# Attention, top-1 experts and a swish layer on one core: transposes of q and k by 64x64 products, norm rounds moved to GpSimd, longer pauses in the gate's queue

## The chip, the cores and the metric

The kernel runs on one core of a Trainium2 chip. The metric is the time of one execution on the device, in microseconds. Before the change the median of three runs is 1353.53 us (1352.38 to 1356.58).

## The reference, cut to what matters

```
x = chunk_attention(q, k, v)          # 8 batches, 8 heads, 576 rows, head size 64; softmax in chunks of 64 rows
x = x.transpose(0, 2, 1, 3).reshape(4608, 512)
xn, en = x / (|x| + 1e-6), emb / (|emb| + 1e-6)
logits = xn @ en.T / tau              # 8 experts
e = argmax(logits); gate_w = softmax(logits)[e]
x = gate_w * (relu(x @ w1[e]) @ w2[e])   # 512 -> 1024 -> 512, one expert for each token
h = x @ w_in;  g = h * sigmoid(1.702 h)  # 512 -> 2048
out = g @ w_out                          # 2048 -> 512
```

All inputs and the output are float32.

## The kernel before, in words

The program has three stages. The attention stage, up to about 264 us of the profile, goes through 36 tiles of 128 token rows in a software pipeline (the loop over `n`, LATE and the dictionaries `front` and `back` set its skew). In step n it transposes k or q of the next 256-row unit on TensorE (`emit_T`, L344, k in even steps, q in odd ones) and copies the result out of the accumulation bank on ScalarE (L349), multiplies q and k of tile n (`emit_S`, L371), subtracts the row maximum on VectorE (L378, L381), takes the exponential on ScalarE (L388), transposes the probabilities of tile n-1 (L394, L401), multiplies by v for tile n-2 (L416) and divides (L424 to L428); for tile n-3 it takes the sum of squares on ScalarE (L436) and splits the row into a high and a low half (`emit_X`: L442 to L452 on VectorE, L454 and L455 on GpSimd), which SyncE stores to a scratch tensor `xs` (L461). Rows are transposed again (L468, L474, L476) and multiplied with the expert embeddings (L491). SyncE also issues the loads of q, k and v, in the program's order, between the stores.

Work on the router is cut into five batches of tiles (8, 8, 8, 6, 6). For each there are two generators in the queue `todo`: `norm` (inverse norms, by three Newton rounds in `rsqrt`, L217 to L230) and `gate` (L560 to L658: logits, maximum, one-hot rows `oh`, their running count by products with a triangle and with ones, L596 to L599, each token's place, and the softmax weight as three small integers). `drip(n)` takes n of their operations (2n in steps 29 to 32, `rate`) and is called ten times a step between the attention's operations on VectorE. After the third batch `order` finds the busiest expert and, by 24 products with one-hot rows (`lookup`, L538), the tokens of its first three tiles; with that known, SyncE loads that expert's weights and VectorE splits them (`first_split`) while the last attention tiles run. A generator that yields "pe" is about to issue a product whose operands were issued on VectorE just before; in the old `drip` the queue then passes over one call at most.

The second stage, to 671 us, runs 39 tiles of 128 gathered tokens through two products in half-precision parts; `mm2_evac` scales a tile's result and packs it, with the token's index and scale in a tail of four 32-bit words, into a row of `ys`. VectorE and ScalarE split the next expert's weights under a branch (`swap`, L962). The third stage, to the end, is the swish layer by seven-product blocks. Both are bound by TensorE.

Of the kernel before, what the change touches and what calls it, by code (L numbers as in the profile page):

```python
# [22 lines left out]
W_EXP = 7  # L23
# [11 lines left out]
def kernel(  # L35
# [173 lines left out]
    sc_i = const.tile([128, MAXT], I32, name="sc_i")  # L209

# [85 lines left out]
    def drip(n):  # L296

        n *= rate[0]
        while n > 0 and todo:
            g = todo[0]  # L300
            if g in paused:
                n -= paused.pop(g)
                continue
            try:
                if next(g) == "pe":
                    paused[g] = 8
                n -= 1
            except StopIteration:
                todo.popleft()
# [195 lines left out]
    def norm(bi):  # L505
        t0, n = batches[bi]
        ssc, y = ss_all[:, t0:t0 + n], rn_all[:, t0:t0 + n]
        yield from rsqrt(y, small("t", n, I32), small("a", n), ssc)
        nc.vector.tensor_tensor(out=y, in0=y, in1=ssc, op=ALU.mult)
        yield  # L510
        nc.vector.tensor_scalar(y, y, 1e-6, None, op0=ALU.add)
        yield
        nc.vector.reciprocal(out=y, in_=y)
        yield
# [3 lines left out]
        )  # L518
        yield
# [25 lines left out]
    def scale_of(cols, got, parts_i):  # L545
# [7 lines left out]
        )  # L553

    def gate(bi):
# [19 lines left out]
        yield  # L575
        w = small("w", n, w=NE)
# [13 lines left out]
        ex = small("ex", n, w=NE)  # L590
        nc.scalar.activation(out=ex, in_=l, func=AF.Exp)
# [42 lines left out]
        if t0 + n == NTILE:  # L634
            yield from flags()
        se = small("se", n)
        nc.vector.tensor_reduce(out=se.unsqueeze(2), in_=ex, axis=AX.X, op=ALU.add)
        yield
        nc.vector.tensor_scalar(se, se, 1e-9, None, op0=ALU.add)
        yield  # L640
        nc.vector.reciprocal(out=se, in_=se)
        yield
        nc.vector.scalar_tensor_tensor(
            out=tok_s[:, T], in0=se, scalar=2.0 ** (-2 * W_EXP), in1=is_all[:, T],
            op0=ALU.mult, op1=ALU.mult,
        )
        yield
        cb = att.tile([128, 3, 8], I32, tag="g_cb", name="g_cb")[:, :, 0:n]
        ci = tok_s[:, T].bitcast(I32)
        nc.vector.tensor_scalar(cb[:, 0], ci, 21, None, op0=ALU.logical_shift_right)  # L650
        yield
        nc.vector.tensor_scalar(
            cb[:, 1], ci, 10, 2047, op0=ALU.logical_shift_right, op1=ALU.bitwise_and
        )
        yield
        nc.vector.tensor_scalar(cb[:, 2], ci, 1023, None, op0=ALU.bitwise_and)
        yield
        nc.vector.tensor_copy(vals[:, 2:5, T], cb)  # L658
        yield
# [41 lines left out]
    def order(c):  # L701
# [42 lines left out]
        yield "pe"  # L744
# [321 lines left out]
    def mm2_evac(i):  # L1066
# [6 lines left out]
        c_i = sc_i[:, i:i + 1]  # L1073
        tail = y[:, 2 * DM:YP].bitcast(I32).rearrange("p (a two) -> p a two", two=2)
        n = (YP - 2 * DM) // 4
# [765 lines left out]
```

## Time and profile before

| | |
|---|---|
| median of 3 runs | 1353.53 us |
| profiled execution | 1351.38 us |
| its span, first to last instruction | 1349.4 us |
| TensorE busy in the span | 1246.7 us (92%) |
| VectorE | 1048.0 us (78%) |
| ScalarE | 732.8 us (54%) |
| GpSimd | 718.4 us (53%) |
| mean granted TensorE clock | 0.976 of full speed |

In the rows, PE is TensorE, PEld its weight loads, DVE VectorE, ACT ScalarE, POOL GpSimd, SP SyncE. A row of a timeline has the start in the span, the length, engine, line, operation, output and inputs; in square brackets stands how long the engine was idle before it and what ended that. Such times are taken by the hardware profiler in one execution.

### The profile page before, as it was taken

The page shows a single profiled execution, that of the slowest core. Times are in us where ns is not written, and L with a number is a line of the kernel's source. Part 1 is how long each engine was busy: PE and PEld are TensorE (multiplying, and loading weights), DVE is VectorE, ACT ScalarE, POOL GpSimd, SP SyncE. Part 2 cuts the span into 40 slices and gives each one's busy share as a digit, 9 for nine tenths or more (in the row PEclk, how much of TensorE's full clock was granted, in tenths as well). Part 3 has the DMA queues.
Part 4 walks back from the last instruction along what each step waited for, and adds up shares of the span by engine and source line. Part 5 has one row for each costly group of instructions (what it writes and reads, how often), then busy time and mean ns, then how long its engine had stood idle before and what let it go on. Part 6 is the DMA issues. An engine that isn't in the chain of part 4 may idle for free. (4 is left out here: it accounts for less than half of the span.)

```text
span 1349.4 us, 35343 instructions
## 1 busy us (share of the span) xinstructions
PE 1246.7 (92%) x14192; PEld 1027.2 (76%) x14192; DVE 1048.0 (78%) x1872; ACT 732.8 (54%) x1301; POOL 718.4 (53%) x652
## 2 busy tenths in 40 slices
PE   6777767899999999999899999999999999999997
PEld 4666656677676666667588888888888888888886
DVE  4688888878988778886678696968687896968681
ACT  7899855235544545554463645545454645455452
POOL 1455543142444254543167575757667675757664
PEclk9999877999999999999999999999999999999999
DMA  9999635668665759885507162544526062534413
GB/s 197 233 242 230 160 129 131 181 181 229 191 182 174 212 161 274 266 253 133 151 15 212 58 183 99 129 154 94 188 39 226 19 205 77 157 125 125 157 42 116
DMA packets 218454, 213.62 MB, mean 158 GB/s; under 512 B 127320, under 2 KB 171352, under 8 KB 218272
## 3 DMA queue, kind: packets, MB, share of 16 engines
q1 hardware_dynamic: 204880, 184.17, 51.0%
q0 software_dynamic: 6000, 19.67, 4.3%
q10 hardware_dynamic: 7392, 7.36, 1.6%
q8 instruction: 114, 1.87, 0.6%
q14 instruction: 68, 0.56, 0.2%
HBM read 154.98 MB, written 36.52 MB: 142 GB/s over the span
## 5 line engine op out<-in xcount | busy, mean ns | idle before, releaser
L1536 PEld LDWEIGHTS <-wS 128*128 128x128 f16 x3024 | 296.2, 98 | 48.9 <-issue 9.7
L1029 PEld LDWEIGHTS <-w1HL 128*128 128x128 f16 x3744 | 216.9, 99 | 24.1 <-DVEq L962 6.7
L1029 PE MATMUL ph<-xTm,w1HL 128*128 128x128 f16 x3744 | 223.0, 222 | 12.2 <-DVEq L962 5.5
L1064 PE MATMUL py<-w2HL,hT 128*128 128x512 f16 x912 | 203.9, 379 | 6.0 <-DVEq L962 3.4
L1064 PEld LDWEIGHTS <-hT 128*128 128x128 f16 x936 | 89.9, 98 | 109.1 <-issue 8.0
L1089 ACT ACTIVATE y<-py,ysc 128x512 f16<-128x512 f32 x38 | 26.1, 687 | 142.8 <-DVE ysc L1086 142.8
L1004 POOL DMA_INDIRECT xg<-xs,id_i x39 | 44.3, 1135 | 107.6 <-DMA xTm<-xg 70.0
L1536 PEld LDWEIGHTS <-w2HL 128*128 128x128 f16 x864 | 84.6, 98 | 10.6
L1536 PEld LDWEIGHTS <-w1HL 128*128 128x128 f16 x864 | 84.5, 98 | 9.8
L454 POOL TENSOR_TENSOR x<-x,sx_all 128x512 f32<-128x512 f32 x33 | 34.3, 1039 | 107.3 <-DVE rd L424 41.9
L1256 POOL TENSOR_TENSOR wS<-d_f,wS 128x512 f16<-128x512 f32 x28 | 37.0, 1339 | 73.4 <-ACT wS L1255 44.5
L1562 ACT ACTIVATE zA<-zA 128x512 f32<-128x512 f32 x72 | 45.3, 628 | 53.2 <-DVE zA L1559 26.9
L1403 POOL TENSOR_TENSOR w1HL<-zA,w1HL 128x512 f16<-128x512 f32 x36 | 48.5, 1346 | 43.6 <-ACT w1HL L1399 39.7
L1396 DVE TENSOR_TENSOR zA<-zA 128x512 f32<-128x512 f32 x72 | 65.6, 910 | 1.2
L1037 DVE SCALAR_TENSOR_TENSOR hT<-ph,hT 128x512 f16<-128x512 f32 x78 | 51.4, 684 | 14.8 <-ACT hT L1036 14.7
L1036 ACT ACTIVATE hT<-ph 128x512 f16<-128x512 f32 x78 | 44.2, 594 | 30.0 <-PE ph L1029 30.0
L1536 PE MATMUL pd<-stg,wS 128*128 128x256 f16 x456 | 54.5, 272 | 2.2 <-ACT stgB L1399 2.2
L1697 POOL DMA_INDIRECT out_dram<-hT,idc x36 | 35.4, 983 | 35.7 <-ACT hT L1692 32.6
L1536 PE MATMUL pa<-stg,wS 128*128 128x256 f16 x432 | 51.7, 273 | 1.5 <-ACT stgB L1399 1.5
L1090 DVE SCALAR_TENSOR_TENSOR y<-py,ysc,y 128x512 f16<-128x512 f32 x38 | 28.5, 751 | 28.8 <-ACT y L1089 28.8
L1536 PE MATMUL pb<-stg,wS 128*128 128x256 f16 x408 | 48.9, 272 | 1.5 <-ACT stgB L1399 1.5
L349 ACT ACTIVATE kuT<-tp 64x512 f32<-64x512 f32 x72 | 45.2, 628 | 8.8 <-PE tp L344 7.9
(408 smaller groups left out, 3134.4 us busy)
## 6 DMA issues: line engine op xcount, KB each, us to landing
ring<-wod SPq DMA_DIRECT2D x63, 1024.0 KB, 5.1
stg<-in_moe_w_dram SPq DMA_DIRECT2D x14, 1024.0 KB, 6.9
stgB<-in_moe_w_dram SPq DMA_DIRECT2D x14, 1024.0 KB, 6.8
ys<-y SPq DMA_DIRECT2D x39, 258.0 KB, 3.2
vt<-in_v_dram SPq DMA_DIRECT2D x64, 144.0 KB, 5.7
xs<-xr SPq DMA_DIRECT2D x36, 256.0 KB, 5.6
raw_o<-in_moe_w_in_dram SPq DMA_DIRECT2D x16, 512.0 KB, 4.3
raw_o<-in_moe_w_out_dram SPq DMA_DIRECT2D x16, 512.0 KB, 3.8
```

The lines of the kernel that those rows point to most:

```text
L349: lambda r=r, p=p, dst=dst: nc.scalar.activation(out=dst[:, :, r], in_=p[r * 64:(r + 1) * 64], func=AF.Copy)
L1004: nc.gpsimd.indirect_dma_start(out=xg[:, :], out_offset=None, in_=src, in_offset=bass.IndirectOffsetOnAxis(ap=id_i[:, i:i + 1], axis=0),)
L1029: nc.tensor.matmul(p[:, f % 4], wt[:, c, fs], xT[:, a, :], start=(c == 0 and a == 0 and wt is w1H), stop=(c == KD - 1 and wt is w1L),)
L1036: nc.scalar.activation(out=hi, in_=p, func=AF.Relu)
L1037: nc.vector.scalar_tensor_tensor(out=lo, in0=p, scalar=0.0, in1=hi, op0=ALU.max, op1=ALU.subtract)
L1064: nc.tensor.matmul(p, hT[:, a, :], wt[:, c, :], start=st, stop=sp)
L1256: nc.gpsimd.tensor_tensor(out=L_, in0=f, in1=H_, op=ALU.subtract)
L1396: nc.vector.tensor_tensor(out=o, in0=x, in1=p, op=op)
L1403: eng.tensor_tensor(out=lo, in0=x, in1=hi, op=ALU.subtract)
L1536: nc.tensor.matmul(dst, lhs(a, k, ab), rhs(b, k), start=first and ab == abs_[0] and k == 0 and m == 0, stop=(k == n - 1 and m == 2), skip_ ...
L1562: nc.scalar.activation(out=z, in_=z, func=AF.Sigmoid, scale=1.702 * 2.0 ** -G_EXP)
L1697: disjoint("out", nc.gpsimd.indirect_dma_start(out=out[:, :], out_offset=bass.IndirectOffsetOnAxis(ap=id_t[j][0][:, 2 * h + t, 0:1], axis= ...
```

## The change

Four parts. The transposes of k and q are now products with a quarter of the identity, 64 rows by 64 columns, ordered so that all of a row half's results lie in one bank; two ScalarE copies of 128 partitions take the place of four of 64. The first four batches' Newton rounds, with the two operations after them, run on GpSimd, and the queue then pauses for eight calls of `drip` (`"far"`); `"pe"` pauses for three. The weight operations of a gate, for all batches but the last, stand right behind the one-hot rows, ahead of the product (`weights`). In `mm2_evac` the tail is written by single-column operations, and the two halves of the token's scale are split once (`sc_m`, `sc_e`) when the scale is found.

```
         n *= rate[0]
         while n > 0 and todo:
             g = todo[0]
-            if g in paused:
-                n -= paused.pop(g)
+            n -= 1
+            if paused.get(g, 0) > 0:
+                paused[g] -= 1
                 continue
             try:
-                if next(g) == "pe":
-                    paused[g] = 8
-                n -= 1
+                r = next(g)
+                if r in ("pe", "far"):
+                    paused[g] = (3 if r == "pe" else 8) * rate[0]
             except StopIteration:
+                n += 1
                 todo.popleft()
...
-        for h2 in range(2):
-            p = ps.tile([128, HP, 128], F32, tag="A", name="tp", bufs=2)
-            for hp in range(HP):
-                nc.tensor.transpose(
-                    p[:, hp, :], src[:, 2 * hp + h2].rearrange("p r d -> p (r d)"), identF
+        p = [ps.tile([128, QR, HP, 64], F32, tag="A", name="tp", bufs=2) for _ in range(2)]
+        for hp in range(HP):
+            for r in range(QR):
+                for a in range(2):
+                    rows = slice(a * 64, (a + 1) * 64)
+                    for h2 in range(2):
+                        nc.tensor.matmul(
+                            p[a][h2 * 64:(h2 + 1) * 64, r, hp, :], src[rows, 2 * hp + h2, r, :],
+                            identF[rows, rows], start=True, stop=True,
+                        )
+        for a in range(2):
+            dst = qkT[u, nm][:, :, a * 128:(a + 1) * 128].rearrange("p hp (i r) -> p hp i r", r=QR)
+            evacs.append([
+                lambda a=a, dst=dst: nc.scalar.activation(
+                    out=dst, in_=p[a].rearrange("p r hp i -> p hp i r"), func=AF.Copy
                 )
-            dst = qkT[u, nm][h2 * 64:(h2 + 1) * 64].rearrange("p hp (c r) -> p hp r c", r=QR)
-            evacs.append([
-                lambda r=r, p=p, dst=dst: nc.scalar.activation(
-                    out=dst[:, :, r], in_=p[r * 64:(r + 1) * 64], func=AF.Copy
-                )
-                for r in range(2)
             ])
...
+        if bi + 1 < len(batches):
+            gp = nc.gpsimd
+            t, a, h = small("t", n, I32), small("a", n), small("h", n)
+            nc.vector.tensor_scalar(t, ssc.bitcast(I32), 1, None, op0=ALU.logical_shift_right)
+            yield
+            nc.vector.tensor_scalar(y.bitcast(I32), t, -1.0, 1597463007.0, op0=ALU.mult, op1=ALU.add)
+            gp.tensor_scalar(h, ssc, -0.5, None, op0=ALU.mult)
+            for _ in range(3):
+                gp.tensor_tensor(out=a, in0=h, in1=y, op=ALU.mult)
+                gp.tensor_tensor(out=a, in0=a, in1=y, op=ALU.mult)
+                gp.tensor_scalar(a, a, 1.5, None, op0=ALU.add)
+                gp.tensor_tensor(out=y, in0=y, in1=a, op=ALU.mult)
+            gp.tensor_tensor(out=y, in0=y, in1=ssc, op=ALU.mult)
+            gp.tensor_scalar(y, y, 1e-6, None, op0=ALU.add)
+            yield "far"
+        else:
+            yield from rsqrt(y, small("t", n, I32), small("a", n), ssc)
...
+        nc.vector.tensor_scalar(
+            sc_m[:, cols], sc_i[:, cols], MAN_BITS, BIAS << 23, op0=ALU.bitwise_and, op1=ALU.bitwise_or
+        )
+        nc.vector.tensor_scalar(sc_e[:, cols].bitcast(I32), sc_i[:, cols], EXP_BITS, None, op0=ALU.bitwise_and)
+        nc.vector.tensor_scalar(
+            sc_e[:, cols], sc_e[:, cols].bitcast(I32), float(BIAS << 23), None, op0=ALU.add
+        )
...
+        if t0 + n < NTILE:
+            yield from weights(T, n, ex)
         yield "pe"
...
-        yield "pe"
+        yield "far"
         p0 = gb[:, 304:304 + 5 * NSURE].rearrange("p (a i) -> p a i", a=5)
         lookup(p0, lambda t: v0[:, :, t], NPART)
...
-        nc.vector.tensor_scalar(si[:, 3:4], c_i, EXP_BITS, None, op0=ALU.bitwise_and)
-        nc.vector.tensor_copy(tail[:, :, 0], id_i[:, i:i + 1].to_broadcast([128, n]))
+        for a in range(0, tail.shape[1], 2):
+            nc.vector.tensor_scalar(tail[:, a:a + 1], id_i[:, i:i + 1], 0, None, op0=ALU.bitwise_or)
...
-        nc.vector.scalar_tensor_tensor(
-            out=si[:, 2:3], in0=c_i, scalar=MAN_BITS, in1=si[:, 1:2], op0=ALU.bitwise_and, op1=ALU.bitwise_or
-        )
+        nc.vector.tensor_scalar(s[:, 2:3], s[:, 1:2], sc_m[:, i:i + 1].bitcast(F32), None, op0=ALU.mult)
...
-        nc.vector.scalar_tensor_tensor(
-            out=tail[:, :, 1], in0=si[:, 3:4].to_broadcast([128, n]), scalar=float(BIAS << 23),
-            in1=si[:, 1:2].to_broadcast([128, n]), op0=ALU.add, op1=ALU.subtract,
-        )
+        for a in range(1, tail.shape[1], 2):
+            nc.vector.tensor_scalar(
+                tail[:, a:a + 1], si[:, 1:2], -1.0, sc_e[:, i:i + 1], op0=ALU.mult, op1=ALU.add
+            )
```

How the order on the engines changes is shown at three places. First VectorE at the third batch's gate, in steps 29 of both programs, from the one-hot rows on (`g_oh`; `g_sm` and `cum` are their counts, `g_se`, `tok_s` and `g_cb` the weight, the rows with `sx_all`, `xr` and `rd` the attention's). Before:

```order
L586 TENSOR_TENSOR g_oh<-g_w,g_mw 128x64
L447 TENSOR_SCALAR sx_all<-si_all 128x1
L452 TENSOR_SCALAR xr<-x,sx_all 128x512
L603 TENSOR_REDUCE g_sm<-g_oh 128x8
L607 TENSOR_TENSOR cum<-cum,g_sm 128x8
L424 TENSOR_SCALAR rd<-db 128x8
L685 TENSOR_TENSOR cnt<-gb,io_eR 128x8
L613 TENSOR_TENSOR g_po<-gb,g_oh 128x64
```

After:

```order
L645 TENSOR_TENSOR g_oh<-g_w,g_mw 128x64
L455 TENSOR_SCALAR sx_all<-si_all 128x1
L588 TENSOR_REDUCE g_se<-g_ex 128x8
L590 TENSOR_SCALAR g_se<-g_se 128x8
L460 TENSOR_SCALAR xr<-x,sx_all 128x512
L592 RECIPROCAL g_se<-g_se 128x8
L594 SCALAR_TENSOR_TENSOR tok_s<-g_se,is_all 128x8
L601 TENSOR_SCALAR g_cb<-tok_s 128x8
L603 TENSOR_SCALAR g_cb<-tok_s 128x8
L432 TENSOR_SCALAR rd<-db 128x8
L607 TENSOR_SCALAR g_cb<-tok_s 128x8
L609 CAST vals<-g_cb 128x3x8
```

The weight operations fill the place behind the one-hot rows, and the counts stand in step 30, behind that step's row maximum.

Second TensorE, from that gate's last products on (`ptp` and `db` are the attention's, `tp` the transposes). Before:

```order
L394 MATMUL ptp<-identF,P 128x128 x4
L416 MATMUL db<-vt_91,PT 64x65 x16
L683 LDWEIGHTS ones_120
L683 MATMUL gb<-cum,ones_120 128x8
L344 MATMUL tp<-identF,ku 128x128 x8
```

After:

```order
L402 MATMUL ptp<-identF,P 128x128 x4
L424 MATMUL db<-vt_91,PT 64x65 x16
L720 LDWEIGHTS ones_120
L720 MATMUL gb<-cum,ones_120 128x8
L351 MATMUL tp<-identF,qu 64x64 x32
```

The gate's products are followed by a transpose of k before and of q after: they moved by one step, to step 30; and eight transposes became 32 calls.

Third GpSimd at the end of the first batch (`x` and `xr` are a tile's two large operations). Before:

```order
L454 TENSOR_TENSOR x<-x,sx_all 128x512
L455 TENSOR_TENSOR xr<-x,xr 128x512
L454 TENSOR_TENSOR x<-x,sx_all 128x512
L455 TENSOR_TENSOR xr<-x,xr 128x512
L454 TENSOR_TENSOR x<-x,sx_all 128x512
```

After:

```order
L462 TENSOR_TENSOR x<-x,sx_all 128x512
L463 TENSOR_TENSOR xr<-x,xr 128x512
L527 TENSOR_SCALAR g_h<-ss_all 128x8
L529 TENSOR_TENSOR g_a<-g_h,rn_all 128x8
L530 TENSOR_TENSOR g_a<-g_a,rn_all 128x8
L531 TENSOR_SCALAR g_a<-g_a 128x8
L532 TENSOR_TENSOR rn_all<-rn_all,g_a 128x8
```

The round L529 to L532 stands there three times, and L533 and L534 behind it, ahead of the next tile's `x`.

## Rows read from the trace of the kernel before

**Rows 1.** busy us (instructions) by stretch: PE, PEld, DVE, ACT, POOL; clock, DMA share, GB/s

```profile
67.40:107.50 40.10, 30.90 (x747) 24.72 (x747) 34.10 (x110) 37.28 (x70) 22.52 (x24) 1.00 1.10 242
107.50:146.50 39.00, 30.75 (x746) 24.65 (x745) 34.18 (x109) 37.11 (x70) 22.52 (x24) 1.00 1.15 234
152.06:188.85 36.79, 24.02 (x499) 20.27 (x494) 28.65 (x99) 23.87 (x45) 15.69 (x18) 0.77 0.17 50
188.85:200.83 11.98, 7.05 (x162) 5.65 (x152) 10.80 (x29) 8.21 (x17) 7.28 (x6) 0.65 0.75 273
264.00:671.00 407.00, 389.75 (x4305) 282.89 (x4306) 329.61 (x569) 196.61 (x337) 163.79 (x137) 0.99 0.70 204
671.00:1349.00 678.00, 658.92 (x5978) 585.00 (x5976) 513.47 (x650) 346.72 (x615) 447.62 (x384) 0.99 0.40 121
```

**Rows 2.** the same view for line L381 alone, one of it per tile

```profile
58.00:152.00 94.00, 13.11 (x19) 1.00 1.12 241
152.06:188.85 36.79, 3.44 (x5) 0.77 0.17 50
188.85:200.83 11.98, 1.38 (x2) 0.65 0.75 273
```

**Rows 3.** issues of transfers, 152 to 187 us: count, size, median us to landing

```profile
xs<-xr SPq DMA_DIRECT2D x5, 256.0 KB, 2.0
```

**Rows 4.** issues of transfers, 60 to 150 us

```profile
xs<-xr SPq DMA_DIRECT2D x19, 256.0 KB, 6.5
```

**Rows 5.** timeline of PE, 150 to 176 us, two rows

```profile
159.55 0.21 PE L596 MATMUL gb<-g_oh,tri 128*128 128x64 f16 x1 [3.37 <-DVE g_oh L586]
...
175.88 0.79 PE L538 MATMUL gb<-v,raw_o 128*128 128x15 f16 x24 [6.06 <-DVE v L740]
```

**Rows 6.** ACT groups, 107.5 to 146.5 us: count | busy us, mean ns | idle

```profile
L349 ACT ACTIVATE quT<-tp 64x512 f32<-64x512 f32 x17 | 10.7, 629 | 0.2
...
L401 ACT ACTIVATE PT<-ptp 128x512 f32<-128x512 f32 x8 | 4.8, 595 | 0.1
L474 ACT ACTIVATE xTa<-sp 128x1024 f16<-128x1024 f16 x4 | 4.1, 1024 | 0.1
```

**Rows 7.** timeline of all engines, 96 to 112 us, two rows

```profile
96.18 0.69 PE L371 MATMUL sp<-kuT,quT 64*64 64x64 f32 x32
...
99.19 0.66 PE L344 MATMUL tp<-identF,ku 128*128 128x128 f32 x4
```

**Rows 8.** DVE groups, 182.6 to 192 us (the fourth batch's norm)

```profile
L230 DVE SCALAR_TENSOR_TENSOR rn_all<-g_a,rn_all 128x6 f32<-128x6 f32 x3 | 1.4, 450 | 0.1
L224 DVE SCALAR_TENSOR_TENSOR g_a<-rn_all,ss_all 128x6 f32<-128x6 f32 x3 | 1.2, 402 | 0.1
...
L228 DVE TENSOR_TENSOR g_a<-g_a,rn_all 128x6 f32<-128x6 f32 x3 | 0.5, 166 | 0.1
...
L511 DVE TENSOR_SCALAR rn_all<-rn_all 128x6 f32<-128x6 f32 x1 | 0.2, 160 | 0.0
L509 DVE TENSOR_TENSOR rn_all<-rn_all,ss_all 128x6 f32<-128x6 f32 x1 | 0.2, 154 | 0.0
```

**Rows 9.** POOL groups over the whole span

```profile
L455 POOL TENSOR_TENSOR xr<-x,xr 128x512 f16<-128x512 f32 x33 | 38.8, 1176 | 2.6
...
L454 POOL TENSOR_TENSOR x<-x,sx_all 128x512 f32<-128x512 f32 x33 | 34.3, 1039 | 107.3 <-DVE rd L424 41.9 <-DVE xr L452 11.0 <-DVE g_t L217 9.8
...
L629 POOL TENSOR_SCALAR raw_o<-io_k,slot 128x128 f16<-128x128 f16 x32 | 20.8, 669 | 19.8 <-DVE slot L626 19.8
...
L1696 POOL MEMSET gap<- 128x1 f32 x36 | 3.8, 106 | 0.0
```

**Rows 10.** lines L1077 and L1078: shortest/median/longest ns, first to last start

```profile
L1077 DVE TENSOR_SCALAR ysc<-sc_i x39: 140/154/154, 241.9 to 661.6; 128x1 int32<-128x1 int32 x39
L1078 DVE COPY y<-id_i x39: 153/159/4056, 242.0 to 661.6; 128x2 int32<-128x2 int32 x39
```

**Rows 11.** waits, 264 to 671 us: total us, times, longest

```profile
PE ph L1029 <- DVEq L962: 5.5, 7, 1.7
```

More of the change, by code (lines that the diff above doesn't have):

```diff
@@ L209 @@
     sc_i = const.tile([128, MAXT], I32, name="sc_i")
+    sc_m = const.tile([128, MAXT], I32, name="sc_m")
+    sc_e = const.tile([128, MAXT], F32, name="sc_e")
     tau_sb = const.tile([128, 1], F32, name="tau_sb")
@@ L507, in norm @@
         ssc, y = ss_all[:, t0:t0 + n], rn_all[:, t0:t0 + n]
[L508 to L514, printed above, removed]
         isx = is_all[:, t0:t0 + n]
@@ L518, in norm @@
         )
+        yield
[3 more added lines that the diff above has]
+            nc.vector.tensor_scalar(t, ssc.bitcast(I32), 1, None, op0=ALU.logical_shift_right)
+            yield
+            nc.vector.tensor_scalar(y.bitcast(I32), t, -1.0, 1597463007.0, op0=ALU.mult, op1=ALU.add)
[10 more added lines that the diff above has]
+            yield from rsqrt(y, small("t", n, I32), small("a", n), ssc)
+            nc.vector.tensor_tensor(out=y, in0=y, in1=ssc, op=ALU.mult)
+            yield
+            nc.vector.tensor_scalar(y, y, 1e-6, None, op0=ALU.add)
+            yield
+        nc.vector.reciprocal(out=y, in_=y)
         yield
@@ L553, in scale_of, with weights @@
         )
+        nc.vector.tensor_scalar(
[5 more added lines that the diff above has]
+        )
+    def weights(T, n, ex):
+        se = small("se", n)
+        nc.vector.tensor_reduce(out=se.unsqueeze(2), in_=ex, axis=AX.X, op=ALU.add)
+        yield
+        nc.vector.tensor_scalar(se, se, 1e-9, None, op0=ALU.add)
+        yield
+        nc.vector.reciprocal(out=se, in_=se)
+        yield
+        nc.vector.scalar_tensor_tensor(
+            out=tok_s[:, T], in0=se, scalar=2.0 ** (-2 * W_EXP), in1=is_all[:, T],
+            op0=ALU.mult, op1=ALU.mult,
+        )
+        yield
+        cb = att.tile([128, 3, 8], I32, tag="g_cb", name="g_cb")[:, :, 0:n]
+        ci = tok_s[:, T].bitcast(I32)
+        nc.vector.tensor_scalar(cb[:, 0], ci, 21, None, op0=ALU.logical_shift_right)
+        yield
+        nc.vector.tensor_scalar(
+            cb[:, 1], ci, 10, 2047, op0=ALU.logical_shift_right, op1=ALU.bitwise_and
+        )
+        yield
+        nc.vector.tensor_scalar(cb[:, 2], ci, 1023, None, op0=ALU.bitwise_and)
+        yield
+        nc.vector.tensor_copy(vals[:, 2:5, T], cb)
+        yield
     def gate(bi):
@@ L575, in gate @@
         yield
+        ex = small("ex", n, w=NE)
+        nc.scalar.activation(out=ex, in_=l, func=AF.Exp)
         w = small("w", n, w=NE)
@@ L589, in gate @@
         yield
-        ex = small("ex", n, w=NE)
-        nc.scalar.activation(out=ex, in_=l, func=AF.Exp)
+        if t0 + n < NTILE:
+            yield from weights(T, n, ex)
         yield "pe"
@@ L635, in gate @@
             yield from flags()
[L636 to L642, printed above, removed]
-        nc.vector.scalar_tensor_tensor(
-            out=tok_s[:, T], in0=se, scalar=2.0 ** (-2 * W_EXP), in1=is_all[:, T],
-            op0=ALU.mult, op1=ALU.mult,
-        )
[L647 to L653, printed above, removed]
-        )
[L655 to L659, printed above, removed]
+        if t0 + n == NTILE:
+            yield from weights(T, n, ex)
         if t0 + n == NPART:
@@ L1092, in mm2_evac @@
         )
-        nc.vector.scalar_tensor_tensor(
-            out=tail[:, :, 1], in0=si[:, 3:4].to_broadcast([128, n]), scalar=float(BIAS << 23),
-            in1=si[:, 1:2].to_broadcast([128, n]), op0=ALU.add, op1=ALU.subtract,
-        )
+        for a in range(1, tail.shape[1], 2):
+            nc.vector.tensor_scalar(
+                tail[:, a:a + 1], si[:, 1:2], -1.0, sc_e[:, i:i + 1], op0=ALU.mult, op1=ALU.add
+            )
         if i < NSURE:
```

5 lines of the change are left out of this document (1 added, 4 removed).

## The prediction

> **What bounds the kernel now.** I read the busy times by stage first. From 671 us to the end TensorE is busy 658.92 of 678 us, from 264 to 671 us 389.75 of 407 [rows 1]: those two stages, 1085 of 1349.4 us, are TensorE's, and what other engines save there is worth at most the 17.25 us that TensorE idles in the first of them. Everything else in the change lies in the attention stage before 264 us. There the reader is to count tiles: the 128-row score subtraction (L381) runs once per tile, 19 times between 58 and 152 us, so a tile takes 94.0 / 19 = 4.95 us; then 5 tiles take 36.79 us (7.36 each) and 2 take 11.98 [rows 2]. These are two regimes.
>
> In the first one I take the two stretches of exactly eight tiles, 67.40 to 146.50 us, 79.1 us together. ScalarE is busy 74.4 of them (94%), VectorE 68.3 (86%), TensorE 61.65 (78%), GpSimd 45.0 [rows 1]. ScalarE sets the pace, but two others are close. The DMA column reads 1.10 and 1.15, 242 and 234 GB/s [rows 1], and a 256 KB store of the token rows, landed 2.0 us after its issue when nothing else is loaded, needs 6.5 us here [rows 3, 4]: the transfers queue behind each other all the time, so I treat some 238 GB/s as what this mix of transfers reaches.
>
> In the second regime no loads of q, k and v are left (50 GB/s) and no engine is near full: VectorE is busy 28.65 of 36.79 us, so it idles 8.1 [rows 1]. The idle time comes from the gate: TensorE, in order, stands 3.37 us before the product over the one-hot rows and 6.06 us before the 24 products that look up the first expert's tokens, each until VectorE is done with a chain that was issued only a few steps earlier [rows 5]; behind that product stand the next tiles' scores, which VectorE needs.
>
> **The change, part by part.**
>
> *q and k by 64x64 products.* Per tile (one of k or q is transposed per tile) four ScalarE copies of 64x512 at 0.629 us [rows 6] become two of 128x512. Nothing in the trace copies from such a strided bank; the nearest rows are 0.595 us for a contiguous 128x512 and 0.629 for the old copy, the far one 1.024 for 128x1024 elements [rows 6]. I take 0.65, with 0.6 and 1.02 as ends: 2.52 - 1.30 = 1.2 us of ScalarE per tile saved (0.5 to 1.3). ScalarE falls from 4.65 to about 3.45 us a tile. On TensorE eight 128x128 passes, 0.66 us per four, so 1.3 us, become 32 calls of 64x64. The score products have that shape and use the same four quarters of the array: 16 calls, shown as 32 matmuls, take 0.69 us [rows 7]. So 32 calls take 1.38: TensorE pays about 0.1 us more, 3.95 a tile. If the quarters did not run beside each other it would be worse; that is a rival below.
>
> *Newton rounds on GpSimd.* Of each of the first four batches' norms eleven VectorE operations go. In the fourth they are 1.4 + 1.2 + 0.5 + 0.2 + 0.2 = 3.5 us [rows 8], 0.44 us a tile: VectorE falls from 4.27 to 3.83. GpSimd gets 15 small operations instead. The trace has no arithmetic on 128x8 there: its memset of 128x1 takes 0.106 us, its compare over 128x128 0.669 [rows 9]. I take 0.2 us, near the small end since eight columns are near one, so 3 us per batch. They stand behind the tile's two large operations (1.04 + 1.18 us [rows 9]), of which about 1.2 us are left when the seed is written, and VectorE's reciprocal comes one tile later: 4.5 - 1.2 = 3.3 us are there for 15 operations, 0.22 each. At 0.2 VectorE waits hardly at all; I charge 0.5 us in all. At 0.669 it would stand 6.7 us in each of three batches (the fourth has two tiles between), 20 us, with the x and score work of every later tile queued behind it. The Trainium skill, page "GPSIMD Engine Reference", section "Engine selection", speaks against this move: it sends elementwise work to VectorE because GpSimd takes about twice as long for two inputs. By that rule an operation takes an estimated 0.33 us instead of VectorE's 0.166, 5 us per batch, 1.7 us of waiting in three batches, and the sum would be 5 us poorer.
>
> *Loads.* With ScalarE at 3.45, VectorE at 3.83 and TensorE at 3.95 the engines would allow about 4.1 us a tile. A tile needs three 256 KB inputs and one 256 KB store, 1.05 MB by the shapes, so at 238 GB/s the transfers need 4.41 us. I take 4.5 us a tile: 19 tiles x (4.95 - 4.5) = **8.5 us** saved. Ends: 0 if the queue of loads already holds the stage, and 19 x (4.95 - 4.1) = 16 if loads issued ahead are enough.
>
> *Real pauses and the moved weight operations.* The same VectorE operations are issued, so nothing of their busy time goes; only waits do. The one-hot product now stands one tile later, the weight operations fill the steps between, and the look-up comes a tile after its operands. What hides it: VectorE always has the attention's own work. Of the 8.1 us of VectorE idle time in the five tiles I count half, 4 us, as gone (0 to 8.1), since the order after the count product is still a chain of small operations. The fourth batch's norm (3.5 us) is also in this VectorE-bound stretch, less three new operations for the split scale, 0.45: 3 us. Together **7 us** (3 to 11). What is late next is VectorE itself: the gate's own operations stay. The last batch keeps its place behind the last row tile, so the start of the expert stage only moves forward with the rest. On SyncE the first expert's weight loads stand behind the same tile's store as before.
>
> *Expert results (mm2_evac).* Seven small operations become eight. The copy of the token index has a median of 159 ns but takes up to 4056; the tensor_scalar just before it, of the form that replaces it, never took over 154 [rows 10]. VectorE gains, TensorE only where it waits for VectorE's branch at a new expert, 5.5 us in 7 waits [rows 11]. I count **0.5 us** (0 to 4).
>
> Sum: -8.5 - 7 - 0.5 + 0.5 = -15.5 us. The profiled execution took 1351.4 us (span 1349.4), the median of the runs is 1353.5, 2.1 above. So 1335.9 for an execution like the profiled one and **1338** beside the median.
>
> **Rivals.**
> 1. *The loads hold the stage.* For: the store's landing is three times the undisturbed one through the whole stretch, and all loads of q and k stand on SyncE ahead of the 23rd tile's store. Against: between 60 and 150 us nothing on TensorE waits for a load. Then the first 150 us give 2 us instead of 8.5, and the sum is -9: 1344.5.
> 2. *Slower: GpSimd's rounds arrive late.* VectorE's reciprocal waits with all attention work behind it. At 0.669 us an operation: 20 us, -15.5 + 20: 1358. It decides from (3.3 + 5.2) / 15 = 0.57 us an operation, where three waits of 5.2 us eat the 15.5. Against: eight columns are far from 128. A kindred price: were the 64x64 calls to run one after the other, TensorE would need over 5 us a tile, and the stage would be some 10 us longer.
> 3. *Nothing is left: VectorE and GpSimd hold each other up.* VectorE's first Newton operation with two inputs takes 0.4 us in the mean against 0.166 for its like, next to running GpSimd work [rows 8]; 15 more GpSimd operations may hold VectorE's others in the same way, up to 3 us in each of four batches, 12 us: 1350. The Trainium skill, "SBUF — State Buffer", section "Who interferes with whom", has the rule: a VectorE operation with two SBUF inputs and a GpSimd one that reads SBUF exclude each other, and the later one stands for the whole of the first. By it the trace's slow first rounds are explained, and this rival's 12 us are the upper end.
> 4. *More than I count.* Loads issued ahead carry the stage at 4.2 us a tile (14 us), and VectorE's idle time in the gate goes almost wholly (10): 1329.
>
> **How the numbers follow.** Forecast 0.50, loads 0.24, slower 0.07, hold-up 0.07, more 0.12. About 0.3%, 4 us, is what a measurement of this kernel can tell from no change, so faster means under 1349.5. Forecast and rival 4 lie there wholly, rival 1 mostly (0.20): 0.82. The same gets the rest of rival 1 and most of rival 3, 0.10; slower 0.08. The range runs from rival 4 to just past rival 1 and to rival 3's 1350: 1328 to 1350; the forecast's own is 1331 to 1345.
>
> **What would show it.** After the change: ScalarE under 80% busy between the 9th and 28th tile, copies of q and k two per tile at about 0.65 us, a tile in 4.3 to 4.7 us there; the 32 calls in about 1.4 us; no TensorE wait over 1.5 us before the one-hot product and the look-up; 15 GpSimd operations of about 0.2 us, and no wait of VectorE's reciprocal on them; the two tiles that now end at 200.83 us done about 13 us earlier; the experts' stage and the last one of equal length. I am wrong if a tile still takes 4.9 us with ScalarE idle (loads), if the reciprocal waits (rival 2), or if the gain before 264 us is given back behind it.

## The result: slower by 13 us

The changed kernel takes 1368.07 us in the median of 4 runs (1365.37 to 1370.42), the kernel before, beside it, 1355.05 (1352.38 to 1357.32): a ratio of 1.0095, 95% interval 1.0075 to 1.0116. The prediction, 1338 us and faster, was wrong. The profiled execution takes 1365.37 us, its span is 1363.6, 14.2 more than before.

### The profile page after: what moved, and what is told of

Its sections match the earlier page's. It is cut to its first block, busy times and chain, and to the rows that moved or that the text cites. A ratio compares the mean times of both kernels' runs of the same rounds, so it can differ in the third digit from the quotient of the medians.

```text
span 1363.6 us, 39324 instructions
## 1 busy us (share of the span) xinstructions
PE 1252.9 (92%) x16208; PEld 1039.0 (76%) x16208; DVE 1023.2 (75%) x1873; ACT 684.9 (50%) x1229; POOL 732.2 (54%) x712
## 5 line engine op out<-in xcount | busy, mean ns | idle before, releaser
L1066 PE MATMUL ph<-xTm,w1HL 128*128 128x128 f16 x3744 | 220.2, 220 | 11.3 <-DVEq L999 7.3
L1569 PEld LDWEIGHTS <-w2HL 128*128 128x128 f16 x864 | 84.5, 98 | 10.6
L386 DVE TENSOR_REDUCE mx<-sp 128x8 f32<-128x512 f32 x36 | 24.7, 686 | 53.9 <-PE sp L379 53.9
```

The costliest lines, as they stand in the source:

```text
L1066: nc.tensor.matmul(p[:, f % 4], wt[:, c, fs], xT[:, a, :], start=(c == 0 and a == 0 and wt is w1H), stop=(c == KD - 1 and wt is w1L),)
L1569: nc.tensor.matmul(dst, lhs(a, k, ab), rhs(b, k), start=first and ab == abs_[0] and k == 0 and m == 0, stop=(k == n - 1 and m == 2), skip_ ...
```

## The profile after

The windows by tile come first, the score subtraction (now L389) alone, one per tile (window, length, busy of VectorE and count, granted clock, DMA share, GB/s). They answer to [rows 2]:

```profile
65.00:173.20 108.20, 13.12 (x19) 0.92 0.87 204
173.20:203.54 30.34, 3.43 (x5) 0.89 0.16 56
203.54:216.76 13.22, 1.38 (x2) 0.76 0.71 249
```

The same 19 tiles take 108.2 us instead of 94.0, 5.7 each; the next five take 30.3 instead of 36.8. So the second regime won 6.4 us, as it should, and the first one lost 14; 7.0 more are lost ahead of it (the window of the same tiles starts at 65.00 instead of 58.00), and the last two tiles lose 1.2. All engines, for 15 tiles of the first regime and for the two later stages (the columns of [rows 1]):

```profile
74.22:114.05 39.83, 30.77 (x1046) 25.79 (x1044) 29.04 (x86) 22.20 (x46) 22.04 (x35) 0.91 0.99 217
114.05:162.20 48.15, 35.25 (x1194) 30.35 (x1194) 32.35 (x98) 27.85 (x56) 26.51 (x41) 0.89 0.80 195
278.00:685.00 407.00, 390.48 (x4338) 283.88 (x4336) 309.70 (x615) 197.84 (x338) 164.10 (x137) 0.99 0.70 205
685.00:1363.00 678.00, 659.68 (x5983) 585.48 (x5980) 514.04 (x650) 346.56 (x615) 448.17 (x384) 0.99 0.40 121
```

The experts and the last stage are as long as before: the experts take 449 us from their first product to their last, 451 before (they begin at 211 us in the kernel before, ahead of the 264 us at which their stage was cut). In the first regime ScalarE fell from 94% busy to 56 and 58%, VectorE from 86 to 73 and 67%, and TensorE too, from 78 to 77 and 73%, with 60% more matmuls. Nothing is full, and the granted clock, 1.00 before, is 0.91 and 0.89. TensorE's busy time per tile rose from 3.85 to 4.40 us at that clock. m1_burst below has TensorE's stops of the kind shown next at a granted clock of 1.00, so a lower clock is not needed for them; what it adds here no run shows. Who waits then, 60 to 165 us (total us, times, longest):

```profile
DVE mx L386 <- PE sp L379: 25.0, 14, 3.8
...
PE tp L351 <- issue: 10.4, 9, 2.4
...
PE sp L379 <- issue: 7.1, 4, 2.5
...
DVE rn_all L542 <- POOL rn_all L534: 1.6, 1, 1.6
```

VectorE waits 25 us for scores, and TensorE stands ahead of transposes and scores with "issue" as the cause: it waits for nothing that the profile shows. One such place in the timeline of TensorE:

```profile
92.69 0.66 PE L402 MATMUL ptp<-identF,P 128*128 128x128 f32 x4
93.27 0.70 PE L424 MATMUL db<-vt,PT 64*64 64x65 f32 x32
93.79 1.05 PE L351 MATMUL tp<-identF,qu 64*64 64x64 f32 x57
97.25 0.34 PE L351 MATMUL tp<-identF,qu 64*64 64x64 f32 x7 [2.41 <-issue]
97.52 0.36 PE L499 MATMUL gb<-enT,xTa 128*128 128x16 f16 x8
```

The reader is to look at x57 and x7: the stop of 2.41 us comes after 57 of the 64 matmuls of one transpose, between two that have the same inputs and the same bank half. No load, buffer or engine can hold the 58th alone. What is left is the instruction itself. The queues of transfers show a kind for that; over 16 tiles (67.4 to 146.5 us before, 74.22 to 166.7 after; packets, MB, share), before and after:

```profile
q8 instruction: 12, 0.20, 1.2%
```

```profile
q8 instruction: 19, 0.31, 1.6%
```

A packet is 16,384 bytes. A tile has 93 matmuls and as many weight loads before, 149 and 149 after: 16 tiles are some 3,000 and 4,780 instructions, so about 250 to a packet (the burst below gives 258; 256 is taken from here on). In the trace's transfer records of the changed kernel they come one after the other, 5.0 us apart between 70 and 150 us (6.5 before). The stops hang on them: between 60 and 165 us TensorE has 19 with "issue" as the cause, 22.2 us together, and each of the 19 ends 1.2 to 1.7 us after the end of such a packet. One packet starts at 94.49 and takes 1.40 us; the stop above ends at 97.25, 1.36 us later. In the kernel before there is no such stop in these tiles.

Of the rest, ScalarE's copies of k and q (shortest/median/longest ns) and GpSimd's small operations are what was expected, 0.58 to 0.60 and 0.20 to 0.24 us:

```profile
L358 ACT ACTIVATE quT<-tp x16: 575/598/606, 74.4 to 165.7; 128x512 f32<-128x512 f32 x16
L358 ACT ACTIVATE kuT<-tp x16: 576/584/597, 77.7 to 161.9; 128x512 f32<-128x512 f32 x16
```

```profile
L531 POOL TENSOR_SCALAR g_a<-g_a 128x8 f32<-128x8 f32 x6 | 1.4, 238 | 0.5
...
L532 POOL TENSOR_TENSOR rn_all<-rn_all,g_a 128x8 f32<-128x8 f32 x6 | 1.2, 202 | 0.5
```

TensorE's waits between 155 and 220 us, to be read against [rows 5]: the two on the one-hot rows and the look-up, 3.37 and 6.06 us, are gone; the longest that are left stand before the products with v and before the logits.

```profile
PE db L424 <- DVE x L436: 7.2, 4, 3.5
PE gb L499 <- ACT xTa L482: 5.3, 1, 5.3
```

The index copy of the experts' results answers to [rows 10] and never takes over 155 ns now; TensorE's wait for VectorE's branch, to [rows 11], is no shorter (7.3 us in 6):

```profile
L1113 DVE TENSOR_SCALAR y<-id_i x78: 136/145/155, 257.9 to 676.0; 128x1 int32<-128x1 int32 x78
```

```profile
PE ph L1066 <- DVEq L999: 7.3, 6, 2.5
```

## The experiments

The leading theory, A: 128 instructions of TensorE a tile in place of 16 need more packets than arrive in time. "Tile" in the table is the distance between the row maxima of the 12th and the 28th tile divided by 16, "six" that from the 30th to the 36th; ratios are to the kernel before on the same chip; the runs are spread over several chips. A tile is read from one profiled execution, and that leaves some 0.1 us open: m1_burst is the kernel before, unchanged, up to its added products, and its tile is 5.07 us where the profile of before has 4.95.

| kernel | median us | ratio, 95% | tile us | six us |
|---|---|---|---|---|
| before | 1355.05 | | 4.95 | 44.5 |
| after | 1368.07 | 1.0095 (1.0075 to 1.0116) | 5.78 | 39.4 |
| x1_old_T | 1349.15 | 0.9966 (0.9953 to 0.9979) | 5.18 | 38.3 |
| x2_new_T | 1375.72 | 1.0154 (1.0130 to 1.0178) | 5.81 | 44.6 |
| x3_16calls | 1346.76 | 0.9954 (0.9938 to 0.9970) | 5.06 | 39.4 |
| x7_after_few_v | 1356.55 | 1.0026 (1.0005 to 1.0047) | 5.41 | 39.4 |
| x6_16calls_few_v | 1341.08 | 0.9899 (0.9874 to 0.9925) | 4.81 | 39.2 |
| x8_mix | 1344.91 | 0.9931 (0.9908 to 0.9954) | 4.95 | 39.3 |
| x9_mix_few_v | 1342.75 | 0.9927 (0.9903 to 0.9950) | 4.93 | 38.2 |
| x10_before_few_v | 1349.80 | 0.9967 (0.9954 to 0.9980) | 4.91 | 45.0 |
| p1_pauses | 1346.34 | 0.9944 (0.9922 to 0.9965) | 5.14 | 38.1 |
| p2_pauses_norms | 1352.91 | 0.9993 (0.9975 to 1.0010) | 5.27 | 39.4 |
| x11_pauses_mix | 1347.24 | 0.9950 (0.9934 to 0.9967) | 5.09 | 38.5 |
| y6_mix_XT_late | 1360.02 | 1.0033 (1.0019 to 1.0047) | 5.67 | 40.5 |
| y7_oldT_XT_late | 1367.45 | 1.0092 (1.0078 to 1.0106) | 6.10 | 40.5 |
| y9_mix_XT_late_few_v | 1357.03 | 1.0019 (1.0006 to 1.0033) | 5.80 | 40.0 |
| y4_mix_xTa_ACT | 1343.63 | 0.9921 (0.9909 to 0.9934) | 4.85 | 37.5 |
| z1_XT_late_xTa_ACT | 1344.93 | 0.9945 (0.9926 to 0.9964) | 5.11 | 37.5 |
| z2_no_gps_norms | 1338.22 | 0.9888 (0.9866 to 0.9910) | 4.93 | 36.3 |

**Without the products, and with nothing else.** x1_old_T puts the old `emit_T` back into the changed kernel, x2_new_T puts the new one alone into the kernel before.

> The changed kernel with q and k transposed as before (8 transposes of 128x128 and four copies per tile); all other parts of the change kept. Theory A (the 32 calls are 128 instructions of TensorE per tile where there were 16, and these arrive too late; TensorE stands with nothing that the profile shows): the stops without a visible cause between 60 and 165 us, some 20 us in the changed kernel, fall under 3 us, a tile takes 4.9 us again, the gate's stretch keeps its 5 us, and the time is 1346 to 1352, a ratio of 0.994 to 0.998. Theory D (GpSimd's rounds, the pauses or the moved weight operations delay the stage): the time stays 1360 to 1370, ratio over 1.004.

> The kernel before with nothing but the 64x64 products for q and k. Theory A: the same stops as in the changed kernel, a tile at 5.6 to 5.9 us instead of 4.95 between the 12th and the 28th, about 20 us lost before 160 us: 1368 to 1378, ratio 1.010 to 1.017. Theory D: no stops, ScalarE relieved: 1342 to 1352, ratio 0.991 to 0.998.

Times and stops are as theory A has them: 0.9966 and 1.0154. The tile of x1_old_T, 5.18 us, is not back at the 4.9 expected, though its stops are gone. The products alone cost 20.8 us, the other three parts together save 4.6; that makes 16.2 where the changed kernel lost 13, which the intervals allow. TensorE's waits, 60 to 150 us, in x2_new_T:

```profile
PE tp L347 <- issue: 6.3, 4, 3.3
PE db L420 <- issue: 4.3, 4, 1.8
PE sp L375 <- issue: 3.5, 2, 2.0
```

In x1_old_T, 60 to 165 us, TensorE has no wait with "issue" as the cause; it waits for ScalarE's copies, as before the change, and for VectorE:

```profile
PE tp L348 <- ACT kuT L353: 7.1, 10, 0.8
PE db L420 <- DVE x L432: 6.9, 7, 1.4
```

**Half the instructions.** x3_16calls keeps the two copies, with 64 instructions a tile:

```
-        for hp in range(HP):
-            for r in range(QR):
-                for a in range(2):
-                    rows = slice(a * 64, (a + 1) * 64)
-                    for h2 in range(2):
-                        nc.tensor.matmul(
-                            p[a][h2 * 64:(h2 + 1) * 64, r, hp, :], src[rows, 2 * hp + h2, r, :],
-                            identF[rows, rows], start=True, stop=True,
...
+        for r in range(QR):
+            p = ps.tile([128, HP, 128], F32, tag="A", name="tp", bufs=2)
+            for hp in range(HP):
+                for h2 in range(2):
+                    nc.tensor.matmul(
+                        p[h2 * 64:(h2 + 1) * 64, hp, :], src[:, 2 * hp + h2, r, :], identF,
+                        start=True, stop=True,
...
```

> The changed kernel with 16 products of 128 rows by 64 columns per tile in place of 32 of 64 by 64: 64 instructions of TensorE instead of 128 (16 before), the same two copies per tile on ScalarE. Theory A (the number of instructions counts): the stops without a visible cause fall from 20 us to under 7, a tile takes 4.6 to 5.1 us, 1345 to 1356, ratio 0.993 to 1.001. Theory B (products in quarters or halves of the array cost TensorE more time than their count says, whatever the number of instructions): a tile stays at 5.6 us or more, 1365 to 1375, ratio over 1.007.

0.9954 and 5.06 us a tile, as theory A expects; TensorE's stops without a cause fall to 2.3 us between 70 and 150 us (17.2 in the changed kernel):

```profile
PE db L419 <- issue: 1.2, 1, 1.2
PE sp L374 <- issue: 1.1, 2, 0.6
```

B falls.

**The cost by itself.** m1_burst runs the products behind the last store, 24 groups of 32 calls in the quiet (L1820), then 24 beside loads:

```
+    burst(24, dst)
...
+    for n in range(18):
+        load_w(NG, n % 7)
+    burst(24, dst)
```

> The kernel before, with the products of the 64x64 transposes measured by themselves behind its last store: 24 groups of 32 calls (128 instructions of TensorE each) with no transfer beside them, then 24 more while eighteen loads of 1 MB run. Theory A: TensorE stands between stretches of some 256 instructions, so a group takes more than the 1.4 us of its matmuls, 1.6 to 2.0 us in the quiet part and over 2.2 us beside the loads; instruction packets of 16 KB come one after the other, one per 256 instructions. Theory B: the matmuls themselves take over 2 us a group in both parts, with no stops. Neither: 1.4 us a group in both parts.

It ran once. The first 24 groups take 42.1 us, 1.75 each, the others 62.4, 2.60 each. Windows in the quiet and beside the loads (columns of [rows 1]), and TensorE's waits ahead of 1384.5 us:

```profile
1343.00:1384.50 41.50, 23.68 (x1423) 21.86 (x1414) 0.00 (x0) 0.00 (x0) 0.00 (x0) 1.00 0.06 16
1386.00:1431.00 45.00, 22.44 (x938) 21.14 (x928) 0.00 (x0) 0.00 (x0) 0.00 (x0) 0.73 1.01 403
```

```profile
PE pd L1820 <- issue: 16.6, 11, 1.9
```

In the quiet TensorE works through 2,837 instructions, 11.1 packets, in 23.68 us, 2.1 us a packet, so a group of 32 calls by itself is 1.07 us; the stops are 11, one per packet. The packets' queue shows 11 in these 41.5 us, 3.7 us apart in the records. Beside 403 GB/s of loads it is 8 in the 43 us from 1388 to 1431, 5.9 us apart in the mean, with stops up to 4.4 us:

```profile
q8 instruction: 8, 0.13, 1.2%
```

So with nothing else to wait for, the packets set the pace, and loads stretch it from 3.7 to 5.9 us. The records show which part they stretch: from TensorE's going on to the start of the next packet it is 1.1 us in the quiet, 2.4 in the changed kernel and 3.7 beside the loads (medians); the packet itself takes 1.1 to 1.2 us and the time from its end to the next instruction 1.2 to 1.7, in all three. A part of the 2.60 us goes with the clock: a group is busy 1.53 us at a granted clock of 0.73 and 1.07 at 1.00. The Trainium skill, page "Runtime: NRT & Kernel Launch", section "Instruction fetch mechanics", says that an engine's instructions are refilled in 16 KiB blocks of 256, and that crossing a block's boundary is "mostly hidden". The trace agrees with the block; on the hiding the measurement decides: 1.5 us per block are not hidden here in the quiet, and more beside loads.

**The changed kernel with a quarter less to load.** x7_after_few_v (and the other few_v kernels):

```
-            nc.sync.dma_start(out=dst, in_=src)
+            if v_n[0] < NV * H:
+                nc.sync.dma_start(out=dst, in_=src)
```

> The changed kernel itself with, of v, only the first three batch entries loaded: a quarter less to transfer per tile. Theory A (TensorE's instructions come by the transfer engines' rings, 3.55 us per packet in the quiet, 6.2 beside full loads): packets come every 4.0 to 4.5 us instead of 4.8, a tile falls from 5.8 us to 4.9 to 5.4, and the time to 1353 to 1362, ratio 0.999 to 1.006, though no engine has less to do. Theory B (the products' shape costs it): a tile stays at 5.6 to 5.8, 1364 to 1370, ratio over 1.007.

The time is as expected of A, some 9 us less than the changed kernel's (1.0026 against 1.0095) with the same work on every engine; the tile, 5.41 us, and the packets, 4.6 us apart, fall as they should and end just past the range written down. The time by itself is weak evidence, since the kernel before gains 4.5 us from the same edit (x10_before_few_v below); the tile and the packets, which came 5.78 and 5.0 us apart, are the better one.

**What the relief of ScalarE is worth, the instructions mended.** x8_mix takes the 16 products for k and the old transposes for q:

```
+    def emit_T(u, nm):
+        return (emit_Tk if nm == "ku" else emit_Tq)(u, nm)
```

> The changed kernel with k by the 16 products of 128 rows by 64 columns and q by the 8 transposes and four copies of before, so that TensorE and ScalarE share the cost. If the engines set the pace of a tile (ScalarE some 4.0 us busy, TensorE 4.3, VectorE 4.0, and at most 40 extra calls), a tile takes 4.5 to 4.75 us between the 12th and the 28th, and the time is 1338 to 1344, ratio 0.988 to 0.993. If the loads of q, k and v hold the stage (rival 1 of the prediction), a tile stays at 4.95 to 5.1 us and the time at 1345 to 1350, ratio 0.994 to 0.998.

> The kernel with 16 products of 128 rows by 64 columns and, of v, only the first three batch entries loaded (later ones compute with these): 0.79 instead of 1.05 MB per tile. If the loads hold the stage, a tile falls from 5.06 us to 4.4 to 4.7, and the time by 6 to 10 us, to 1336 to 1341, ratio 0.988 to 0.992. If the engines do (TensorE 4.6 us busy per tile), a tile stays at 4.85 to 5.1 and the time at 1343 to 1348.

> The kernel that has k by 16 products and q by 8 transposes, with only the first three batch entries of v loaded: of the 18.6 MB that it moves between 70 and 146 us about 4.5 MB go. No engine of it is over 88% busy there. If the transfers hold a tile at 4.95 us (18.6 MB at 245 GB/s are 76 us), it falls to 4.35 to 4.65 us, and the time to 1335 to 1341, ratio 0.986 to 0.990. If the chain from engine to engine holds it, the tile stays at 4.8 to 4.95 and the time at 1341 to 1346.

> The kernel before with only the first three batch entries of v loaded. If ScalarE (94% busy) sets the pace of a tile, as the prediction has it, the tile stays at 4.8 to 4.95 us and the time at 1349 to 1354, ratio 0.996 to 1.0. If the transfers do, it falls to 4.65 to 4.75, as far as ScalarE's 4.65 us allow, and the time to 1344 to 1349, ratio 0.993 to 0.996.

x8_mix has one stop without a cause between 70 and 150 us, of 0.3 us, and no engine over 88% busy, and yet the tile is 4.95, the upper of the two outcomes written down, where loads were held to be the cause; its time lies between the two. The loads are not it: x9_mix_few_v moves 172 instead of 245 GB/s, and its tile is 4.93. The same window, 70 to 146 us, of x8_mix and x9_mix_few_v:

```profile
70.00:146.00 76.00, 66.57 (x1616) 53.55 (x1614) 64.70 (x191) 62.22 (x119) 49.18 (x69) 1.00 1.12 245
```

```profile
70.00:146.00 76.00, 65.98 (x1618) 53.59 (x1620) 65.63 (x192) 62.72 (x120) 49.43 (x71) 1.00 0.62 172
```

x10_before_few_v says the same of the kernel before: 4.91, as with ScalarE as its bound; that its time falls by 4.5 us all the same is not explained, and its profiled execution, the slowest of its ten, shows no stage shorter. Of the two kernels with fewer instructions than the change, x6_16calls_few_v alone gains from fewer loads (0.9899 against 0.9954, and 4.81 against 5.06 us a tile), but its instructions, 0.9 packets a tile, can arrive sooner too, so it does not tell the two apart.

That 4.95 us is also the tile of the kernel before does not mean that the relief is worth nothing, since x8_mix holds the other parts of the change as well. The kernel that differs from it in the transposes alone is x1_old_T: 5.18 us a tile and 0.9966 against 0.9931, some 5 us, with intervals that just overlap. The same edit between p1_pauses and x11_pauses_mix, below, takes 0.05 us off the tile and nothing off the time. So the relief won 0.05 to 0.23 us a tile where 0.45 were counted.

**The parts of the router.** p1_pauses has the real pauses and moved weight operations alone; p2_pauses_norms adds the rounds on GpSimd (`norm` of the change); x11_pauses_mix adds the shared transposes to p1_pauses.

> The kernel before with the real pauses and the moved weight operations alone: no GpSimd rounds, no 64x64 products, results of the experts as before. By the prediction's terms: 4 us from the waits of the gate's stretch, the fourth norm's 3 us not: 1348 to 1351, ratio 0.996 to 0.998, the stretch of six tiles from 44.5 to 40 to 42 us. If the gain of 4.6 us that the changed kernel without the products shows is the norms' instead, this one stays within 0.2% of before.

> The real pauses and moved weight operations with the Newton rounds of the norms on GpSimd. By the prediction's terms (the fourth norm's 3 us off VectorE, 0.5 us of waiting in all) 2 to 3 us better than the pauses alone, 0.992 to 0.993. If GpSimd's rounds hold VectorE's reciprocal up by 1.6 us per batch, as the traces show in places, no better or up to 3 us poorer: 0.994 to 0.997.

> The real pauses and moved weight operations with k by 16 products and q by 8 transposes; the norms and the experts' results as before. If the gains of the two parts add (pauses alone 0.9944, transposes shared between the engines some 4 us on top), 1339 to 1344, ratio 0.989 to 0.993. If the transfers hold the stage whatever the engines do, no better than the pauses alone: 1344 to 1348.

The pauses save 7.6 us (4.7 to 10.6), more than was expected, with 44.5 us of the six tiles down to 38.1. With the rounds on GpSimd most of it is lost: 0.9944 becomes 0.9993, intervals apart, and poorer than either outcome written down. VectorE's waits up to 250 us in p2_pauses_norms hold a row that p1_pauses hasn't:

```profile
DVE rn_all L536 <- POOL rn_all L528: 5.0, 3, 1.9
```

Three waits of 1.6 to 1.9 us with the attention's work queued behind them. The 15 small operations, most of them 0.20 to 0.26 us, take 4.6 us from the start of the first to the end of the last, so 0.3 each with the time between them. But x1_old_T has the same waits,

```profile
DVE rn_all L538 <- POOL rn_all L530: 4.8, 3, 1.6
```

and comes to 0.9966. It differs from p2_pauses_norms in the experts' results alone, and there its profile is no shorter (452 against 450 us from the first to the last product of the experts). So either the experts' results win some 3 us that the profile does not show, or the loss between p1_pauses and p2_pauses_norms is in part scatter; no run settles it. x11_pauses_mix is no better than the pauses alone, the second outcome written down; its loads theory does not follow, since x9_mix_few_v has shown the loads not to hold the tile.

**Is it one chain?** In x8_mix the trace shows a loop around the score banks: maximum, subtraction, copy of the transposed rows, logits, row transposes, scores. y6, y7 and y9 put copy, logits and row transposes elsewhere; y4 makes every such copy on ScalarE; z1 does both.

```
-        while late:
-            end_L(late.popleft())
...
-        if n in front:
-            emit_XT(front[n])
         on(n, emit_S, max_S)
-        if n in front:
-            evac_XT(front[n])
-            turned.append(front[n])
+        while late:
+            end_L(late.popleft())
...
         on(n - 2, emit_x)
+        if n in front:
+            emit_XT(front[n])
+            evac_XT(front[n])
+            turned.append(front[n])
```

```
-        if t >= 30 or t % 2:
+        if True:
             nc.scalar.activation(out=xv, in_=xtp, func=AF.Copy)
```

> The kernel with k by 16 products and q by 8 transposes, in which the transposes of the token rows and the copy of them stand behind the tile's row scale instead of ahead of its score products, and the logits behind the score products. Theory C (a tile is held at 4.95 us by one chain around the score banks, by the trace: row maximum 0.68, subtraction 0.69, copy of the transposed rows 0.68 or 1.02, logits 0.36, the next row transposes 0.61, score products 0.69, 3.7 to 4.1 us and six hand-overs): with the copy, the logits and the row transposes off the chain a tile takes 4.4 to 4.7 us, and the time is 1335 to 1341, ratio 0.986 to 0.990. Theory V (VectorE, 4.2 us busy a tile and never free in time, sets the pace): a tile stays at 4.85 to 5.0 and the time at 1342 to 1347.

> The same later place of the row transposes and the logits, with q and k transposed by the 8 transposes and four copies of before. By theory C ScalarE, 4.65 us busy a tile, is the next bound: a tile takes 4.7 to 4.85 us, the time is 1340 to 1346, ratio 0.990 to 0.994, and some 4 us above the kernel that shares the transposes between the engines. Theory V: 5.1 us a tile as without the move, 1347 to 1351.

> The kernel with k by 16 products and q by 8 transposes, in its old order, with every copy of the transposed rows on ScalarE (1.02 us) where VectorE makes every second (0.68): 0.34 us less a tile for VectorE, 0.5 more for ScalarE (4.55). Theory V: a tile falls to 4.6 to 4.8 us, 1338 to 1343, ratio 0.989 to 0.992. Theory C: the chain of every second tile is 0.34 us longer, so a tile takes 5.0 to 5.2, 1344 to 1350, ratio 0.993 to 0.997.

> The kernel with the later row transposes and shared transposes of q and k, with only the first three batch entries of v loaded. If, the chain being broken, the transfers hold the stage next (1.19 MB a tile at 245 GB/s are 4.85 us), a tile is 0.2 to 0.4 us shorter than with all of v, and the time 4 to 7 us less. If the engines hold it, the same tile within 0.1 us and the same time within 3 us.

> The kernel with the later row transposes, and every copy of the transposed rows on ScalarE, so that the score products no longer wait for VectorE's copy (17 us of TensorE's time between 70 and 146 us in the run without this). Theory C (the chain around the score banks holds the tile, and that new wait hid it): 4.5 to 4.75 us a tile, 1337 to 1343, ratio 0.987 to 0.992. If TensorE's own row of products has become the pace (4.3 and 5.0 us for the two kinds of tile, with no product left to fill its waits): 4.9 to 5.2 us a tile, 1343 to 1350.

y6 and y7 missed both theories: the copy, now last in VectorE's queue, holds the next scores (TensorE's waits in y6, 70 to 146 us):

```profile
PE sp L397 <- DVE xTa L502: 17.0, 7, 3.6
```

y9 shows once more that it is not the loads: its tile is 5.80 us against the 5.67 of y6. The chain, theory C, falls: y4 takes 4.85 us where 5.0 to 5.2 was due, and z1, freed of the new wait, 5.11 where 4.5 to 4.75 was. VectorE's queue as the pace, theory V, is neither shown nor excluded: 4.85 is 0.05 us above its range, less than one profile tells apart. z1's tile and its 1344.9 us lie in the range written down for TensorE's own row of products as the pace; no run tests that alone. So what holds a tile at 4.85 to 5.1 us once the instructions arrive stays open. It is not the loads, and ScalarE alone only in small part.

**The best of it.** z2_no_gps_norms: y4 with the norms back on VectorE.

> The kernel with k by 16 products, q by 8 transposes and every copy of the transposed rows on ScalarE, in the old order, with the norms' Newton rounds back on VectorE; real pauses, moved weight operations and the results of the experts as in the change. If GpSimd's rounds cost what the pair of runs with the pauses says (about 5 us), 1337 to 1341, ratio 0.986 to 0.990. If VectorE's 3.5 us per batch weigh as much as GpSimd's waits, 1341 to 1346, ratio 0.991 to 0.994, no different from the kernel with the rounds on GpSimd.

1338.2 us, 0.9888: 14.3 us faster than the kernel before and better than y4 (0.9921, from another chip; the intervals just touch). That points the same way as the pair with the pauses, but does not show it: in the two profiles the 36th tile comes at 190.9 us here and at 190.4 in y4, so the attention stage is no shorter.

## Why the prediction was wrong

- **The failed step: "So 32 calls take 1.38: TensorE pays about 0.1 us more".** As time on the array this was too high, not too low: 1.07 us in the quiet burst. The price is in the count. The prediction took the durations of the calls from a row and left out their number: 299 instructions a tile are 1.17 packets. The trace of before had a packet every 6.5 us; at its pace of 4.95 us a tile the change asks for one every 4.2, and beside the loads they came every 5.0. (That 1.17 times 5.0 us is the tile measured proves nothing by itself, since packets come as instructions are used up; the 19 stops that end behind packets, x3_16calls and m1_burst do.) Where 8.5 us were to be saved, x2_new_T lost 20.8.
- **The kindred price in rival 2** ("were the 64x64 calls to run one after the other", some 10 us) had the right place and sign, by luck: its mechanism was another. Rival 2 proper, late GpSimd rounds, happened at a quarter to a third of its 20 us.
- **"The engines would allow about 4.1 us", "the transfers need 4.41".** ScalarE fell as predicted and its copies were 0.59, not 0.65. But with the instructions mended a tile stays at 4.95 (x8_mix), 0.23 us less than with the old transposes beside the same other parts (x1_old_T), and where the norms are as before 0.05 less (x11_pauses_mix against p1_pauses); 0.45 were counted. The 1.05 MB a tile were counted from shapes; the queues move 18.6 MB in 16 tiles, 1.16. That would have made the loads the bound, and x9_mix_few_v shows that they are not. Busy shares of 94, 86 and 78% did not say what a tile falls to when the first is relieved.
- **Real pauses and weight operations: right in place and sign, near the upper end in size.** 4 us were counted (0 to 8.1), p1_pauses gives 7.6; the two long waits are gone.
- **Norms on GpSimd: no gain, and by one pair a loss.** Most operations take the 0.20 to 0.26 us that "0.2" stood for, but the sum left out the time between them: 15 take 4.6 us, not 3, and reach VectorE 1.6 to 1.9 us late three times, where 0.5 us in all was charged. The estimate that the prediction set aside, "1.7 us of waiting in three batches" and a sum 5 us poorer, is what the trace shows. Instead of 3 us won some 6.6 are lost between p1 and p2; the waits are 5.0 of them, and that they cost as much is not shown (x1_old_T).
- **Experts' results:** 0.5 us (0 to 4) was counted; not settled. The index copy's long cases are gone, TensorE's wait is not; x1_old_T, which has this part, is 0.0027 below p2_pauses_norms, which lacks it, with intervals that just overlap.

## What to carry to other kernels

Count instructions, not only their time: when an edit replaces few large TensorE calls by many small ones, divide the instructions of a tile by 256 and compare with the packets in the queue of kind "instruction": in this kernel one took 3.7 us in the quiet and 5 to 6 beside loads. A stop with cause "issue" in the middle of a run of equal matmuls that ends 1.2 to 1.7 us behind such a packet is the sign, and it grows beside saturated loads. An engine that is 94% busy is not thereby the only pace: relieve it alone in a trial, and measure that trial against the kernel that differs in nothing else, before counting on the gain.

## What the runs showed of the hardware that was not expected

- A packet of 256 TensorE instructions per 3.7 us in the quiet and per 5.9 us beside 403 GB/s of loads, where TensorE needs 2.1 us to work through one. What the loads lengthen is the time before the packet starts, 1.1 to 3.7 us, not the packet.
- The granted clock stayed at 1.00 (2.4 GHz) through the quiet burst with its 11 stops of up to 1.9 us; beside the loads, with stops of up to 4.4 us, its mean was 0.73, between the two levels.
